# Three half tiles of an attention turned on VectorE, later stores of prepared weights, and banks planned to stay longer, in one core's attention with two MLPs

## The chip, the core and the metric

The kernel runs on one core of a Trainium2 chip. The metric is the device time of one execution in microseconds (us). The engines are TensorE (PE in the profile), VectorE (DVE), ScalarE (ACT), GpSimd (POOL) and SyncE (SP), which here only issues DMAs. ACT issues some DMAs too (ACTq in the rows).

## The reference

A two-stage attention feeds two gated MLPs; all of it is float32.

```python
def sm_attn(qq, kk, vv):                       # softmax attention, scale 1/8
    s = scale * np.matmul(qq, kk.transpose(0, 1, 3, 2))
    a = np.exp(s - np.max(s, axis=-1, keepdims=True))
    return np.matmul(a / (np.sum(a, axis=-1, keepdims=True) + 1e-09), vv)
# q, k, v: 8 batches x 8 heads x 576 x 64; p: 8 x 8 x 32 x 64
p_packed = sm_attn(p, k, v)
out = sm_attn(q, p_packed, p_packed)
x = out.transpose(0, 2, 1, 3).reshape(4608, 512)
x = silu(x @ w_in) @ w_out                     # 512 -> 2048 -> 512
x = hardswish(x @ w_in2) @ w_out2              # 512 -> 2048 -> 512, h * clip(h + 3, 0, 6) / 6
```

## The kernel before

**Tiles and blocks.** The attention is cut into 16 tiles, each of half a batch's heads; of q, k and v each tile has two half tiles of 128x512 values. The first MLP runs in nine blocks (`block`). In a block, `hidden(j, f, ...)` makes one of 16 groups of 128 hidden columns (PE lines L992 to L994, each float32 product being three passes: high by high, high by low, low by high), ACT applies SiLU (L1001) and makes its high half `gh` (L1008), VectorE the rest `gl` (L1009), and `project` (L1016 to L1018) multiplies them into four accumulators. The attention steps of coming tiles are run between these products. The second MLP runs last, from about 810 us to the end, with nothing else beside it.

**What orders the attention steps.** `Plan` counts products as its time. Each step has a due time and, if it needs PSUM, a number of banks out of a ring of four (`bank=`); `give` puts the bank back after an estimated hold. After the exponentials of a tile the plan takes it that banks come free later, by `LATE` = 24 (L820). So the order of all engines' work is fixed when the program is built; at run time an instruction only waits for what it needs.

**The attention steps that matter here.** `load_nat` (L367) loads the half tiles of q, k and v. `step_tr` (L451) turns one half tile of q or k: for tiles 0 to 3 by four PE transposes into one bank (L449) and an ACT copy out of it (T, L108), for tiles from 4 on by one VectorE transpose (L456). For that form the half tile has to lie otherwise in SBUF, so `load_nat` loads it by four DMAs of 32x16x32 values, 64 KB each, in place of two of 128x4x64 values, 128 KB each. The four are put in the list `due` and issued by `ask`; in blocks 0 and 1 `use` issues all that is in it at once. `step_kpq` turns the exponentials (L413, and T copied by ACT), and `step_pp` (L482, L485) multiplies them with v.

**Block 0** (about 36 to 145 us) also converts the first MLP's weights. For each group of w_in or w_out an ACT-issued DMA (`load_raw`, L155, 512 KB) brings the raw words; ACT (L180, L186), VectorE (L195, L199) and POOL (L208) turn the words into float32; ACT casts the high half (`conv_hi`, L219) and VectorE subtracts for the low half (`conv_lo`, L224), both into a tile `win` or `wo`. PE uses this tile in block 0, and SP stores it to DRAM for the later blocks (`keep`, L215, `w1i<-win` and `w1o<-wo`). There are three buffers for `win`: the cast of a group waits until the store of the group three before it has landed.

**DMA queues.** SP issues its DMAs in the program's order; so does ACT, between its other instructions. In the compiled program the DMAs of SP and ACT together take eight completion semaphores in turn, and an instruction that issues a DMA first waits until the DMA that had the semaphore before, eight issues earlier, has landed, unless another wait already implies it.

**Later blocks** read the stored weights back (`wi<-w1i` L247, `wo<-w1o` L260) and prepare the second MLP's weights: `Prep.all` works through 32 units, a `yield` at a time, each ending in three SP stores (L340 to L342) of the tiles `hi` and `c`, of which there are two buffers each.

Of the kernel before, what the change touches and what calls it, by code (L numbers as in the profile page):

```python
# [18 lines left out]
def tile_pack_attention_two_mlps(ctx: ExitStack, tc, q, k, v, p, w_in1, w_out1, w_in2, w_out2, out):  # L19
# [8 lines left out]
    nc = tc.nc  # L28
# [4 lines left out]
    P = 128  # L33
# [124 lines left out]
    def win_src(w, f):  # L158
        return w.bitcast(I32)[:, 2 * f * P:2 * (f + 1) * P].rearrange("(a p) f -> p a f", p=P)

    def wout_src(w, f):
        return w.bitcast(I32)[f * P:(f + 1) * P, :].rearrange("p (a f) -> p a f", a=1)
# [26 lines left out]
    def conv_begin(key, room=ring):  # L189
        conv_a(key, room)  # L190
        conv_b(key, room)

    def conv_shift(key):
        r = raws[key][1]
        nc.vector.tensor_scalar(out=r, in0=r, scalar1=3, scalar2=None, op0=ALU.logical_shift_left)  # L195

    def conv_sign(key):
        w1, r, t = raws.pop(key)
        nc.vector.scalar_tensor_tensor(out=r, in0=w1, scalar=-0x80000000, in1=r, op0=ALU.bitwise_and, op1=ALU.bitwise_or)  # L199
        raws[key] = r, t  # L200

    def conv_bits(key):
        conv_shift(key)
        conv_sign(key)
# [64 lines left out]
    class Prep:  # L269


        def __init__(self, pool, w_in, w_out_):
            self.pool = pool
            self.src = {"in": lambda f: win_src(w_in, f), "out": lambda f: wout_src(w_out_, f)}
            self.units = [(kind, f, h) for kind in ("in", "out") for f in range(HF) for h in range(2)]
            self.steps = self.all()

        def room(self):
# [22 lines left out]
        def all(self):  # L301
            self.load(0)
            for _ in range(6):
                yield
            for u, (kind, f, h) in enumerate(self.units):
                key = "p", u
                c = self.pool.tile([P, 8, P], F32, tag="c8", name="c8", bufs=2)
                hi = self.pool.tile([P, S7, P], F32, tag="hi7", name="hi7", bufs=2)
                conv_begin(key, self.room)
                yield  # L310
                yield
                conv_bits(key)
                yield
                if u + 1 < len(self.units):
                    self.load(u + 1)
                yield
                x, r = raws.pop(key)
                a = c[:, 0:4].bitcast(I32)
                if kind == "in":
                    x, r, a = x, r, a.rearrange("p n f -> p (n f)")  # L320
                else:
                    x, r = (t.rearrange("p (b r f) -> p b r f", b=8, r=2) for t in (x, r))
                    a = a.rearrange("p (r n) (b f) -> p (n b) r f", n=2, b=4)
                nc.gpsimd.tensor_add(out=a, in0=x, in1=r)
                yield

                nc.vector.tensor_add(out=c[:, 4], in0=c[:, 2], in1=c[:, 3])
                nc.vector.tensor_sub(out=c[:, 6], in0=c[:, 0], in1=c[:, 2])
                nc.vector.tensor_sub(out=c[:, 5], in0=c[:, 4], in1=c[:, 0])
                nc.vector.tensor_sub(out=c[:, 7], in0=c[:, 1], in1=c[:, 5])  # L330
                yield
                nc.scalar.copy(out=hi[:, 0:2].bitcast(F32R), in_=c[:, 0:2])
                nc.scalar.copy(out=hi[:, 2:7].bitcast(F32R), in_=c[:, 3:8])
                yield
                nc.gpsimd.tensor_sub(out=c[:, 0:2].bitcast(F32R), in0=c[:, 0:2], in1=hi[:, 0:2])
                nc.gpsimd.tensor_sub(out=c[:, 3:8].bitcast(F32R), in0=c[:, 3:8], in1=hi[:, 2:7])
                yield
                yield
                to = w2[kind][f].rearrange("s p f -> p s f")
                nc.sync.dma_start(out=to[:, :, h * P:(h + 1) * P], in_=hi)  # L340
                nc.sync.dma_start(out=to[:, 0:2, (2 + h) * P:(3 + h) * P], in_=c[:, 0:2])
                nc.sync.dma_start(out=to[:, 2:7, (2 + h) * P:(3 + h) * P], in_=c[:, 3:8])  # L342


    AHEAD = 3
# [5 lines left out]
    def ask(key=None):  # L351
        while due if key is None else any(k == key for k, _ in due):
            due.pop(0)[1]()
            if key is None:
                return
# [11 lines left out]
    def load_nat(n, what, j):  # L367
        src = {"k": k, "q": q, "v": v}[what]
        b, h0 = n // QPB, (n % QPB) * HQ + 2 * j
        m = half_kb(n, "nat", 2 * AHEAD, what)  # L370
        rows = src[b, h0:h0 + 2, 0:T, :]
        if what == "v":
            m = m.rearrange("p (h i d) -> p h i d", h=2, i=NI)
            load_queue[0].dma_start(out=m.rearrange("p h i d -> p h (i d)"), in_=rows.rearrange("h (p i) d -> p h (i d)", i=NI))
        elif n >= 4:

            g = m.rearrange("p (i b d) -> p i b d", i=NI, b=NI)
            for h in range(2):
                for e in range(2):
                    o = (2 * h + e) * NP  # L380
                    src = rows[h].rearrange("(b r i) d -> r i b d", b=NI, i=NI)[:, :, :, e * NP:(e + 1) * NP]
                    due.append(((what, n, j), lambda to=g[o:o + NP], src=src: nc.sync.dma_start(out=to, in_=src)))
        else:
            m = m.rearrange("p (i h d) -> p i h d", h=2, i=NI)
            for h in range(2):
                load_queue[0].dma_start(out=m[:, :, h, :], in_=rows[h].rearrange("(p i) d -> p i d", i=NI))
            m = m.rearrange("p i h d -> p i (h d)")
        nat[what, n, j] = m
# [58 lines left out]
    def turn_rows(ps, m):  # L447
        for i in range(NI):
            nc.tensor.transpose(ps[:, i * P:(i + 1) * P], m[:, i, :], ident)  # L449

    def step_tr(n, what, j):  # L451
        m = nat.pop((what, n, j))
        if n >= 4:
            ask((what, n, j))
            t = half_kb(n, "T", 5)
            nc.vector.transpose(out=t, in_=m)  # L456
            st[what, n, j] = t
            return
        ps = bank()
        turn_rows(ps, m)  # L460
        t = half_kb(n, "T", 5)
        copy(out=t, in_=ps)
        st[what, n, j] = t
# [260 lines left out]
    for j in range(2, B - 1):  # L724
        c, d = QPB * (j + 2), QPB * (j + 1)
# [26 lines left out]
    def use(what, n):  # L752
        used.add((what, n))
        load_next()
        while due and plan.block < 2:
            ask()
# [8 lines left out]
    class Plan:  # L765
# [40 lines left out]
        def run(self, step):  # L806
            self.steps.remove(step)
            _, key, cost, fn, _, tile, bank, count, also = step
            fn()
            self.now += cost  # L810
            for k in (key, *also):
                self.open.discard(k)
                self.done[k] = self.now
            if tile:
                self.tiles.append(tile)
            if bank:
                self.take(count)
                self.give(bank, count)
            if key[0] == "exps":
                self.late = self.now + LATE  # L820

        def tick(self, n, part, calm=False):
            self.now += n
# [16 lines left out]
    LATE = 24  # L840
# [3 lines left out]
    def window(c, d, b, a, j, x):  # L844
# [6 lines left out]
        def add(n, what, cost, fn, *need, tile=None, bank=5, also=(), count=1):  # L851
            if n is not None:
                steps.append(((what, n), cost, fn, need, tile, bank, [k for k in also if k[1] is not None], count))
# [30 lines left out]
        add(c, "spread", 0, lambda: spread_p(c), ("kpq", b), bank=0)  # L884

        def turn():
            add(d, "q0", 0, lambda: step_tr(d, "q", 0), (("t", b if j == 1 else None), 0), bank=5 if j == 0 and (d or 9) < 4 else 0, tile=("z", d))
            add(d, "q1", 0, lambda: [step_tr(d, "q", 1), use("q", d)], ("q0", d), bank=5 if j == 0 and (d or 9) < 4 else 0, tile=("z", d))
            add(a, "u", 0, lambda: [step_u(a), step_ut(a)], before[1], (("t", b), 22 if j else 0), bank=15)
            add(c, "k0", 0, lambda: step_tr(c, "k", 0), (("q1", d), 0), (("t", b if j == 1 and d is not None else None), 20), bank=5 if j == 0 and (c or 9) < 4 else 0, tile=("s", c))  # L890
            add(c, "k1", 0, lambda: [step_tr(c, "k", 1), use("k", c)], ("k0", c), bank=5 if j == 0 and (c or 9) < 4 else 0, tile=("s", c))

        if j == 0:
            if b is not None:
# [11 lines left out]
        else:  # L906
            p = pend.pop() if pend else None
# [11 lines left out]
            if keys:  # L919
                n_banks = (b is not None) + (p0 is not None) + 1  # L920
                add(keys[0][1], keys[0][0], 2 * n_banks, transposes, before[0] if b is not None else ("spread", c), ("spread", c), ("pp", p0), tile=b is not None and ("pp", b),
                    bank=8, count=n_banks, also=keys[1:])
# [13 lines left out]
            if keys:  # L936
# [3 lines left out]
                    bank=9, also=keys[1:], count=n_banks)  # L940
# [935 lines left out]
    for j in range(NBLK):  # L1876
        ws = WINDOWS[j] if j < len(WINDOWS) else []
        order = []
        n = QPB * (j + 1) - 1
# [13 lines left out]
        if j in mates:  # L1893
            for g in range(1, NG):
                fs = fuse_steps(j, g)
                lo, hi = [max(0, 18 * g * GF - 24) / (18 * NF) for g in (g - 1, g)]
# [101 lines left out]
```

## Time and profile before

| | |
|---|---|
| median of 3 runs (lowest to highest) | 1508.78 us (1508.05 to 1509.45) |
| profiled execution, its own time | 1509.61 us |
| its span in the trace | 1507.8 us |
| mean granted clock of TensorE | 0.995 of full speed |
| PE busy | 1483.1 us, 98% of the span |
| DVE / ACT / POOL busy | 1036.0 / 779.4 / 192.5 us |
| PE busy in 70:76 and 114:120 | 3.68 and 3.70 of 6.00 us |

A row of a timeline reads: start, duration (us), engine, line, operation, output<-input, and in square brackets the idle time of the engine just before it with what ended it. Several equal instructions in a row stand as one (x4). A matmul's duration is longer than its share of the engine, since matmuls overlap: the distance between starts tells what one costs. For a DMA issue (SPq, ACTq) the duration is that of issuing, not of the transfer; of several issues, their waits in between are in it.

### The profile page before, as it was taken

The page shows a single profiled execution, that of the slowest core. Times are in us where ns is not written, and L with a number is a line of the kernel's source. Part 1 is how long each engine was busy: PE and PEld are TensorE (multiplying, and loading weights), DVE is VectorE, ACT ScalarE, POOL GpSimd, SP SyncE. Part 2 cuts the span into 40 slices and gives each one's busy share as a digit, 9 for nine tenths or more (in the row PEclk, how much of TensorE's full clock was granted, in tenths as well). Part 3 has the DMA queues.
Part 4 walks back from the last instruction along what each step waited for, and adds up shares of the span by engine and source line. Part 5 has one row for each costly group of instructions (what it writes and reads, how often), then busy time and mean ns, then how long its engine had stood idle before and what let it go on. Part 6 is the DMA issues. An engine that isn't in the chain of part 4 may idle for free.

```text
span 1507.8 us, 21726 instructions
## 1 busy us (share of the span) xinstructions
PE 1483.1 (98%) x7550; PEld 1230.3 (82%) x7550; DVE 1036.0 (69%) x1695; ACT 779.4 (52%) x1241; POOL 192.5 (13%) x177
## 2 busy tenths in 40 slices
PE   7999999999999999999999999999999999999998
PEld 4777777777777778788878888888888888999998
DVE  6767466756575656653463779786978687778767
ACT  6876657655566456655452344334433443444443
POOL 2433011111211211123240000000000000000000
PEclk9999999999999999999999999999999999999999
DMA  9999789997698769868895576678667866997987
GB/s 246 306 306 276 247 214 253 274 253 198 177 245 263 199 165 306 231 178 239 243 291 178 193 225 216 195 216 252 219 193 223 242 215 210 286 313 255 271 273 226
DMA packets 434509, 358.52 MB, mean 238 GB/s; under 512 B 191200, under 2 KB 325856, under 8 KB 434400
## 3 DMA queue, kind: packets, MB, share of 16 engines
q1 hardware_dynamic: 422832, 343.59, 77.6%
q10 hardware_dynamic: 11568, 13.54, 2.9%
q8 instruction: 61, 1.00, 0.3%
q14 instruction: 48, 0.39, 0.1%
HBM read 295.17 MB, written 61.87 MB: 237 GB/s over the span
## 4 chain that ended last, share of the span: by engine, by line
PE 84%; ACT 6%; DMA 4%; DVE 3%; SPq 2%; issue 1%; POOL 1%; ACTq 0%; POOLq 0%; DVEq 0%
PE b L1270 8%; PE b L1268 8%; PE b L1269 8%; PE b L1363 8%; PE b L1366 7%; PE b L1365 7%; PE acc L1016 7%; PE acc L1017 7%; PE acc L1018 7%; PE hps L992 4%; PE hps L993 4%; PE hps L994 4%; DMA wo<-w1o 1%; DMA praw<-in_moe_w_out_dram 1%; PE abank L524 1%
## 5 line engine op out<-in xcount | busy, mean ns | idle before, releaser
L1009 DVE TENSOR_TENSOR gl<-hps,gh 128x512 fp32r<-128x512 f32 x144 | 98.9, 687 | 190.6 <-ACT gh L1008 187.8
L1366 PE MATMUL b<-ro,ws 128*128 128x512 f32 (+2 forms) x564 | 206.4, 366 | 0.0
L1365 PE MATMUL b<-ro,ws 128*128 128x512 f32 (+2 forms) x564 | 206.3, 366 | 0.0
L1268 PE MATMUL b<-xc,ws 128*128 128x512 f32 (+1 forms) x560 | 205.7, 367 | 0.0
L1270 PE MATMUL b<-xc,ws 128*128 128x512 f32 (+1 forms) x560 | 205.7, 367 | 0.0
L1269 PE MATMUL b<-xc,ws 128*128 128x512 f32 (+1 forms) x560 | 205.7, 367 | 0.0
L1311 DVE TENSOR_TENSOR ro<-g,ro 128x1024 fp32r<-128x1024 f32 (+1 forms) x140 | 161.5, 1158 | 41.5 <-ACT ro L1306 41.2
L1306 ACT CAST ro<-g 128x1024 fp32r<-128x1024 f32 (+1 forms) x140 | 132.0, 967 | 93.4 <-DVE g L1299 34.5
L1001 ACT ACTIVATE hps<-hps 128x512 f32<-128x512 f32 x144 | 83.9, 583 | 116.0 <-PE hps L994 115.0
L1363 PE MATMUL b<-ro,ws 128*128 128x512 f32 (+2 forms) x564 | 138.9, 367 | 0.3
L1366 PEld LDWEIGHTS b<-ro,ws 128*128 128x128 f32 x564 | 105.9, 188 | 13.1
L1365 PEld LDWEIGHTS b<-ro,ws 128*128 128x128 f32 x564 | 105.9, 188 | 13.1
L1268 PEld LDWEIGHTS b<-xc,ws 128*128 128x128 f32 x560 | 105.1, 188 | 13.2
L1269 PEld LDWEIGHTS b<-xc,ws 128*128 128x128 f32 x560 | 105.1, 188 | 13.2
L1016 PE MATMUL acc<-gh,wo 128*128 128x512 f32 x288 | 114.6, 398 | 1.3 <-DMA wo<-w1o 1.3
L1270 PEld LDWEIGHTS b<-xc,ws 128*128 128x128 f32 x560 | 105.1, 188 | 13.0
L1363 PEld LDWEIGHTS b<-ro,ws 128*128 128x128 f32 x564 | 102.9, 188 | 15.0 <-DVE ro L1311 2.1
L1016 PE MATMUL acc<-gh,wr 128*128 128x512 f32 x288 | 114.0, 396 | 0.5 <-ACT gh L1008 0.5
L1017 PE MATMUL acc<-gl,wr 128*128 128x512 f32 x288 | 112.5, 391 | 0.2 <-DVE gl L1009 0.2
L1018 PE MATMUL acc<-gh,wr 128*128 128x512 f32 x288 | 112.5, 390 | 0.0
L1018 PE MATMUL acc<-gh,wo 128*128 128x512 f32 x288 | 112.4, 390 | 0.0
L1017 PE MATMUL acc<-gl,wo 128*128 128x512 f32 x288 | 112.4, 390 | 0.0
(310 smaller groups left out, 2899.4 us busy)
## 6 DMA issues: line engine op xcount, KB each, us to landing
ws<-w2in SPq DMA_DIRECT2D x280, 256.0 KB, 3.3
ws<-w2out SPq DMA_DIRECT2D x280, 256.0 KB, 3.5
wi<-w1i SPq DMA_DIRECT2D x80, 512.0 KB, 6.6
wo<-w1o SPq DMA_DIRECT2D x64, 512.0 KB, 6.2
x1d<-x SPq DMA_DIRECT2D x18, 512.0 KB, 5.2
w1i<-win SPq DMA_DIRECT2D x16, 512.0 KB, 7.2
praw<-in_moe_w_in_dram SPq DMA_DIRECT2D x32, 256.0 KB, 6.2
praw<-in_moe_w_out_dram SPq DMA_DIRECT2D x32, 256.0 KB, 5.7
```

The source lines that it names most:

```text
L1009: nc.vector.tensor_sub(out=gl, in0=g, in1=f32(gh))
L1016: mm(acc[e], lhsT=w[:, 0, s], rhs=gh, start=first, stop=False)
L1017: mm(acc[e], lhsT=w[:, 0, s], rhs=gl, start=False, stop=False)
L1018: mm(acc[e], lhsT=w[:, 1, s], rhs=gh, start=False, stop=last)
L1268: mm(ps, lhsT=wh, rhs=xs[k][:, 0, c], start=first, stop=False, skip_group_check=True)
L1269: mm(ps, lhsT=wh, rhs=xs[k][:, 1, c], start=False, stop=False, skip_group_check=True)
L1270: mm(ps, lhsT=wl, rhs=xs[k][:, 0, c], start=False, stop=last, skip_group_check=True)
L1306: nc.scalar.copy(out=t[:, 0], in_=v)
L1311: nc.vector.tensor_sub(out=t[:, 1], in0=self.operand(s), in1=f32(t[:, 0]))
L1363: mm(to, lhsT=wh, rhs=x, start=False, stop=last, skip_group_check=True)
L1365: mm(to, lhsT=wh, rhs=x, start=first, stop=False, skip_group_check=True)
L1366: mm(to, lhsT=wl, rhs=x, start=False, stop=False, skip_group_check=True)
```

## The change

There are three parts.

1. q and k of tile 3 and q of tile 2 (six half tiles) are loaded by the four small DMAs each and turned on VectorE, as tiles 4 and up are. They need no bank any more. k of tile 2 stays on PE.
2. In `Prep.all` the three stores at the end of a unit are kept in a list and issued in the next unit, two `yield`s after its start.
3. After the exponentials of a tile in block 0 whose second exponential is none (the key's third entry is `None`), the plan takes banks to come free after 34 instead of 24.

```diff
@@ class Prep, all()
-                key = "p", u
+                key, after = ("p", u), self.after
                 conv_begin(key, self.room)
                 yield
                 yield
+                for fn in after:
+                    fn()
                 conv_bits(key)
...
                 to = w2[kind][f].rearrange("s p f -> p s f")
-                nc.sync.dma_start(out=to[:, :, h * P:(h + 1) * P], in_=hi)
-                nc.sync.dma_start(out=to[:, 0:2, (2 + h) * P:(3 + h) * P], in_=c[:, 0:2])
-                nc.sync.dma_start(out=to[:, 2:7, (2 + h) * P:(3 + h) * P], in_=c[:, 3:8])
+                self.after = [lambda o=o, i=i: nc.sync.dma_start(out=o, in_=i) for o, i in (
+                    (to[:, :, h * P:(h + 1) * P], hi), (to[:, 0:2, (2 + h) * P:(3 + h) * P], c[:, 0:2]), (to[:, 2:7, (2 + h) * P:(3 + h) * P], c[:, 3:8]))]
+            for fn in self.after:
+                fn()
@@ load_nat
-        elif n >= 4:
+        elif n >= 3 or (what, n) == ("q", 2):
@@ step_tr
-        if n >= 4:
+        if n >= 3 or (what, n) == ("q", 2):
@@ Plan.run
-                self.late = self.now + LATE
+                self.late = self.now + (34 if key[2] is None and not self.block else LATE)
@@ turn (q1 and k1 alike)
-            add(d, "q0", 0, lambda: step_tr(d, "q", 0), ..., bank=5 if j == 0 and (d or 9) < 4 else 0, tile=("z", d))
+            add(d, "q0", 0, lambda: step_tr(d, "q", 0), ..., bank=0, tile=("z", d))
-            add(c, "k0", 0, lambda: step_tr(c, "k", 0), ..., bank=5 if j == 0 and (c or 9) < 4 else 0, tile=("s", c))
+            add(c, "k0", 0, lambda: step_tr(c, "k", 0), ..., bank=5 if j == 0 and c == 2 else 0, tile=("s", c))
```

Lines after L276 have moved by one to four: L449, L482, L485 and L992 of before are L453, L486, L489 and L996 of the changed kernel, L382 (a small load) is L386, and L386 (a load of 128x4x64) is L390.

On PE, in block 0 between two projects (72 to 81 us in the trace of before), there stood before, `nat` being a half tile of q or k as loaded, `abank` a PSUM bank, `T` turned rows:

```order
L449 MATMUL abank<-ident,nat 128x128 x4
L992 MATMUL hps<-xh_546,win 128x512
L993 MATMUL hps<-xl_553,win 128x512
L994 MATMUL hps<-xh_546,win 128x512
L992 MATMUL hps<-xh_559,win 128x512
L993 MATMUL hps<-xl_561,win 128x512
L994 MATMUL hps<-xh_559,win 128x512
L482 MATMUL abank<-nat,T 32x64 x16
L485 MATMUL abank<-vt,a1Tt 32x64 x4
L449 MATMUL abank<-ident,nat 128x128 x8
L992 MATMUL hps<-xh_563,win 128x512
```

and now:

```order
L996 MATMUL hps<-xh_555,win 128x512
L997 MATMUL hps<-xl_557,win 128x512
L998 MATMUL hps<-xh_555,win 128x512
L996 MATMUL hps<-xh_559,win 128x512
L997 MATMUL hps<-xl_563,win 128x512
L998 MATMUL hps<-xh_559,win 128x512
L486 MATMUL abank<-nat,T 32x64 x16
L489 MATMUL abank<-vt,a1Tt 32x64 x4
L1020 MATMUL acc_578<-gh,wr_886 128x512
```

All transposes of this place are gone (four more stood in the project behind it), and pp of tile 2 (L482, now L486) has moved behind the last part of the hidden group. The other place that loses transposes, 110 to 119 us, loses two groups of four.

On SP, at the start of block 0 (30 to 50 us), there stood before, `nat<-in_q_dram` being the load of q of tile 2, `nat<-in_k_dram` that of k of tile 3, `w1i_117<-win` the stores of converted w_in:

```order
L386 DMA nat<-in_q_dram 128x4x64 x4
L155 DMA raw<-in_moe_w_in_dram 128x4x256
L393 DMA pn<-in_p_dram 128x64
L155 DMA raw_233<-in_moe_w_out_dram 128x1024
L215 DMA w1i_117<-win 256x4x128
L386 DMA nat<-in_k_dram 128x4x64 x4
L215 DMA w1i_117<-win 256x4x128
```

and now:

```order
L155 DMA raw<-in_moe_w_in_dram 128x4x256
L397 DMA pn<-in_p_dram 128x64
L155 DMA raw_229<-in_moe_w_out_dram 128x1024
L386 DMA nat<-in_q_dram 32x16x32 x5
L215 DMA w1i_117<-win 256x4x128
L386 DMA nat<-in_q_dram 32x16x32 x3
L386 DMA nat<-in_k_dram 32x16x32 x8
L215 DMA w1i_117<-win 256x4x128
```

Eleven loads stand between the first two weight stores, where there were four.

Also on SP, at 78 to 96 us, `nat<-in_q_dram` being q of tile 3 and `nat<-in_k_dram` k of tile 4, before:

```order
L374 DMA nat<-in_v_dram 128x2x256 x2
L386 DMA nat<-in_q_dram 128x4x64 x4
L382 DMA nat<-in_k_dram 32x16x32 x8
L215 DMA w1o_123<-wo 128x2x512
L215 DMA w1i_119<-win 256x4x128 x2
```

and now:

```order
L378 DMA nat<-in_v_dram 128x2x256 x2
L386 DMA nat<-in_q_dram 32x16x32 x8
L386 DMA nat<-in_k_dram 32x16x32 x8
L215 DMA w1o_123<-wo 128x2x512
L215 DMA w1i_119<-win 256x4x128 x2
```

Sixteen loads stand ahead of the next weight stores, where there were twelve. In the compiled program the DMA ahead of which a queue has to wait for a landing changes with them: before the `w1o_123` store of the changed kernel SP waits for the raw load that ACT issues last before it (at 95.66 us in the trace of before), while before it waited for one of the k loads.

On VectorE six transposes `T<-nat` are new (four around 75 to 83 us, two around 110 to 120 us), on ACT six copies `T<-abank` are gone. In blocks 1 to 8 each group of three stores of part 2 stands later on SP by one to some twenty DMAs; the group at 224 us stands now behind the next tile's loads of v, q and k, which it stood ahead of.

## Rows read from the trace of the kernel before

**Rows 1.** The page, part 1: busy time of each engine.

```profile
PE 1483.1 (98%) x7550; PEld 1230.3 (82%) x7550; DVE 1036.0 (69%) x1695; ACT 779.4 (52%) x1241; POOL 192.5 (13%) x177
```

**Rows 2.** PE's waits, whole span: line <- what ended them: total us, times, longest.

```profile
PE abank L449 <- DVE gl L1009: 4.6, 2, 2.3
PE abank L482 <- DMA nat<-in_v_dram: 1.7, 2, 0.9
```

**Rows 3.** Timeline of PE, first place with transposes.

```profile
74.32 0.66 PE L449 MATMUL abank<-ident,nat 128*128 128x128 f32 x4 [2.32 <-DVE gl L1009]
...
76.88 1.08 PE L482 MATMUL abank<-nat,T 128*32 128x64 f32 x32
...
81.33 0.40 PE L1018 MATMUL acc<-gh,wr 128*128 128x512 f32 x1
...
82.24 0.39 PE L1017 MATMUL acc<-gl,wr 128*128 128x512 f32 x1
...
83.39 0.39 PE L992 MATMUL hps<-xh,win 128*128 128x512 f32 x1
```

**Rows 4.** Windows: PE, PEld, DVE, ACT, POOL busy (count), granted clock, DMA share, GB/s.

```profile
76.00:82.00 6.00, 6.00 (x65) 4.59 (x63) 4.19 (x8) 5.24 (x10) 2.87 (x2) 0.75 0.87 278
```

**Rows 5.** Timeline of DVE, both places.

```profile
73.58 0.69 DVE L1009 TENSOR_TENSOR gl<-hps,gh 128x512 fp32r<-128x512 f32 x1 [1.09 <-ACT gh L1008]
...
117.77 0.69 DVE L1009 TENSOR_TENSOR gl<-hps,gh 128x512 fp32r<-128x512 f32 x1 [1.56 <-ACT gh L1008]
```

**Rows 6.** Groups by line: count, busy us, mean ns of one, idle before.

```profile
L456 DVE STREAM_TRANSPOSE T<-nat 128x512 f32<-128x512 f32 x48 | 31.6, 688 | 2.3 <-DMA nat<-in_k_dram 2.3
```

**Rows 7.** Timeline of SP, 30 to 48 us.

```profile
30.82 2.63 SPq L386 DMA_DIRECT2D nat<-in_q_dram  x4
...
41.40 5.89 SPq L386 DMA_DIRECT2D nat<-in_k_dram  x4
47.39 0.62 SPq L215 DMA_DIRECT2D w1i<-win  x1
```

**Rows 8.** Timeline of ACT and its queue, 48 to 75 us.

```profile
48.08 0.34 ACTq L155 DMA_DIRECT2D raw<-in_moe_w_out_dram  x1
...
54.82 0.62 ACT L219 CAST win<-cr 128x512 fp32r<-128x512 f32 x1 [1.09 <-DMA w1i<-win]
...
74.17 0.58 ACT L108 COPY T<-abank 128x512 f32<-128x512 f32 x1
```

**Rows 9.** DMA issues of 48.05:48.3: count, KB each, us from issue to landing.

```profile
raw<-in_moe_w_out_dram ACTq DMA_DIRECT2D x1, 512.0 KB, 6.3
```

**Rows 10.** Timeline of PE, later hidden groups and the second pp.

```profile
57.93 0.39 PE L992 MATMUL hps<-xh,win 128*128 128x512 f32 x1
...
108.11 0.39 PE L992 MATMUL hps<-xh,win 128*128 128x512 f32 x1
...
120.93 1.08 PE L482 MATMUL abank<-nat,T 128*32 128x64 f32 x32
```

**Rows 11.** Timeline of SP, 82 to 97 us.

```profile
82.94 8.99 SPq L382 DMA_DIRECT2D nat<-in_k_dram  x8
92.49 1.92 SPq L215 DMA_DIRECT2D w1o<-wo  x1
94.50 1.78 SPq L215 DMA_DIRECT2D w1i<-win  x2
```

**Rows 12.** Timeline of ACT and its queue, 92 to 105 us.

```profile
92.25 0.62 ACT L219 CAST wo<-cr 128x512 fp32r<-128x512 f32 x1 [1.45 <-DMA nat<-in_k_dram]
...
95.66 0.39 ACTq L155 DMA_DIRECT2D raw<-in_moe_w_in_dram  x1
...
103.52 0.39 ACTq L155 DMA_DIRECT2D raw<-in_moe_w_in_dram  x1
103.95 0.62 ACT L219 CAST win<-cr 128x512 fp32r<-128x512 f32 x1 [2.78 <-POOL cr L208]
```

**Rows 13.** DMA issues of 94.4:94.6, columns as in group 9.

```profile
w1i<-win SPq DMA_DIRECT2D x1, 512.0 KB, 9.0
```

**Rows 14.** Timeline of SP, stores of part 2 and the loads behind them.

```profile
227.23 2.32 SPq L342 DMA_DIRECT2D w2in<-c  x1
229.76 0.60 SPq L364 DMA_DIRECT2D vt<-in_v_dram  x1
230.42 1.64 SPq L374 DMA_DIRECT2D nat<-in_v_dram  x2
```

More of the change, by code (lines that the diff above doesn't have):

```diff
@@ L275, in __init__ @@
             self.units = [(kind, f, h) for kind in ("in", "out") for f in range(HF) for h in range(2)]
+            self.after = []
             self.steps = self.all()
@@ L886, in turn @@
         def turn():
-            add(d, "q0", 0, lambda: step_tr(d, "q", 0), (("t", b if j == 1 else None), 0), bank=5 if j == 0 and (d or 9) < 4 else 0, tile=("z", d))
-            add(d, "q1", 0, lambda: [step_tr(d, "q", 1), use("q", d)], ("q0", d), bank=5 if j == 0 and (d or 9) < 4 else 0, tile=("z", d))
+            add(d, "q0", 0, lambda: step_tr(d, "q", 0), (("t", b if j == 1 else None), 0), bank=0, tile=("z", d))
+            add(d, "q1", 0, lambda: [step_tr(d, "q", 1), use("q", d)], ("q0", d), bank=0, tile=("z", d))
             add(a, "u", 0, lambda: [step_u(a), step_ut(a)], before[1], (("t", b), 22 if j else 0), bank=15)
-            add(c, "k0", 0, lambda: step_tr(c, "k", 0), (("q1", d), 0), (("t", b if j == 1 and d is not None else None), 20), bank=5 if j == 0 and (c or 9) < 4 else 0, tile=("s", c))
-            add(c, "k1", 0, lambda: [step_tr(c, "k", 1), use("k", c)], ("k0", c), bank=5 if j == 0 and (c or 9) < 4 else 0, tile=("s", c))
+            add(c, "k0", 0, lambda: step_tr(c, "k", 0), (("q1", d), 0), (("t", b if j == 1 and d is not None else None), 20), bank=5 if j == 0 and c == 2 else 0, tile=("s", c))
+            add(c, "k1", 0, lambda: [step_tr(c, "k", 1), use("k", c)], ("k0", c), bank=5 if j == 0 and c == 2 else 0, tile=("s", c))
         if j == 0:
```

## The prediction

> **What bounds the kernel now.** I read the busy times first: PE works 98% of the span [rows 1], so nearly everything that the change can gain is PE idle time or PE work that goes away, and what it can lose is new idle time of PE. Next, PE's waits. The two largest behind the start, and the two that the change aims at, are 4.6 us in front of transposes (L449), two times 2.3 us, both ended by VectorE's gl, and 1.7 us in front of pp for v [rows 2]. Then the timelines of those places, and last, since DMAs are what the change adds, SP and ACT's queue in block 0. There the reader is to see that SP's stores of converted weights decide when ACT may go on: its cast of 54.82 waited 1.09 us for a store issued at 47.39 [rows 7, 8].
>
> **Part 1, what it takes away.** One group of four transposes costs PE 82.24 − 81.33 = 0.91 less two matmul steps of 0.23, so 0.455 us [rows 3]; six groups make 2.7 us. The stalls: in front of L449 PE idles until 74.32 because the bank is the one that gl reads, which ends at 73.58 + 0.69 = 74.27 [rows 3, 5]. pp takes over that bank's place and also needs T, copied by ACT until 74.17 + 0.58 = 74.75 [rows 8]. So pp can start at 74.8 in place of 76.88. Between the start of pp and the next hidden group at 83.39 lie 6.51 us; of these the transposes go (at least 3 × 0.455 = 1.37), and the hidden part that now stands ahead of pp (3 × 0.23 = 0.68): 4.46 remain, the group starts at 79.3, 4.1 us earlier. In the second place gl ends at 118.46 and T, by the first place, 0.48 later, at 118.95, against pp at 120.93 [rows 5, 10]: 2.0 us, and 2.5 with the ACT copy (0.58) that is gone ahead of it. If nothing else came later, part 1 would give 4.1 + 2.5 = 6.6 us. The clock adds little: it was 0.75 after the stall [rows 4], but the remaining wait for T is nearly as long, so I count nothing, with 0.5 us either way in the range.
>
> VectorE gets six transposes of 0.688 [rows 6], 4.1 us; ACT loses six copies of about 0.58, 3.5 us. VectorE waited 1.09 and 1.56 us for ACT just in front of the two gl that count [rows 5], which is what hides them; without that cover one transpose in front of pp's end would cost 0.7. I count nothing.
>
> **Part 1, what it puts in the way.** The loads cost twice the issues. On SP the four loads of q of tile 2 took 2.63 us, 0.66 each [rows 7]; eight small ones of k took 8.99, 1.12 each with their waits [rows 11]. Two stores stand behind them.
>
> *First store.* Before, k of tile 3 was issued from 41.40 on in four DMAs, which ended only at 47.29, since the last waited for the landing of a raw load (the eight semaphores), and the store followed at 47.39 [rows 7]. In the changed program this same wait stands ahead of the second of eleven loads, and a later one, for ACT's raw load of 48.08, ahead of k's sixth. That raw load landed at 48.08 + 6.3 = 54.4 [rows 8, 9]. Three loads follow, 0.66 to 1.12 each: the store goes at 56.4 to 57.8, and with the 7.4 us that it took before (47.39 to the cast it released at 54.82) lands at 63.8 to 65.2. ACT's cast goes from 54.82 to about 64, so ACT is late by D = 9. Bounds: ten more loads than before lie between the first landing and the store; at 0.66 and with no second landing to wait for they make 6.6, at 1.12 they make 11.2; I take 5.5 to 11. PE has only 57.93 − 55.44 = 2.5 us of slack to this cast [rows 8, 10]; it idles for the other 6.5. ACT has next to no idle time until T at 74.17 to make it good, at most 1 us, so pp starts at 74.8 + 8 = 82.8, and the group of 83.39 at 87.3: minus 4.1 has become about +4 us. Queued behind the store on SP are p, k's tail and the next weight stores; behind the waiting cast on ACT, the raw loads, SiLU and the exponentials.
>
> *Second store.* Before `w1o` SP waited for a k load and issued at 92.49, then `w1i` at 94.50 [rows 11]. That landed 9.0 later, at 103.5 [rows 13], which is when ACT's queue, and then its cast, went on (103.52, 103.95) [rows 12]: this store already sets ACT's pace. Now `w1o` has to wait for ACT's raw load of 95.66 to land. That load was itself held by SP (the 1.45 us of idle at 92.25 [rows 12]), so alone it might go at 95.2; with PE late by 4 it goes at about 99. Plus 6.3 (the raw load's landing) is 105.3, `w1i` 0.7 to 2.0 later at 106.5, landing 9.0 later at 115.5 (7.4, as the other store: 113.9). The cast of 103.95 comes at 115.5, 11.5 late. PE has 108.11 − 104.57 = 3.5 us of slack there [rows 10, 12], so it stalls again. From that cast to gl ACT shows no idle time, only the copy that is gone, so pp comes at 118.95 − 0.58 + 11.5 = 129.9, against 120.93: block 0 ends 9 us later, the 6.6 us being in this already. Bounds: with D = 5.5, the raw load at 96 and the shorter times the landing is at 110.4, pp at 124.8, +4; with D = 11 and a 9.0 us landing, +11. I take +8, a little under the middle working, since ACT has some idle time between 85 and 95 and loses four copies there.
>
> After this PE has no stall in which it could make time good: the rest of block 0 and all that follows shifts as a whole.
>
> **Part 2.** The three stores waited on SP for ACT and POOL; at 224 us the last of them took 2.32 us at 227.23, and v was issued behind them only at 230.42 [rows 14]. pp stalled 1.7 us for that v [rows 2]. In the new order v stands ahead of the stores, so this goes: −1.7. The stores wait less, since their tiles have long been ready; queued behind them now are praw and wo loads, and `hi` and `c`, with two buffers each, come free later, by one unit out of two. Nearest rows for a harm: the same two waits of 0.8 us, moved to another load. Bounds: −3 to +1.7. I take −1.7.
>
> **Part 3** moves no work but pp of tile 2 behind one hidden part, which is counted above.
>
> **Sum.** +8 − 1.7 = +6.3 us on the profiled execution's 1509.61; the median is 0.8 lower, so 1508.8 + 6.3 = 1515. Its own range is 1508 (+4 − 3 − 2 for what I may have missed in ACT's recovery) to 1521 (+11 + 1.7).
>
> **Rivals.**
> *The issues hide (A).* If the loads and the raw landings ahead of the two stores are over as early as before, ACT is not delayed and part 1 gives its 6.6: 1508.8 − 6.6 − 1.7 = 1500.5, faster. It decides at the first store: ACT's cast may slip 2.5 us before PE idles, so the store would have to go by 50. For it: SP had no more than 0.66 us per load when nothing waited, and the 5.89 us of [rows 7] were mostly waiting. Against: the waits are for landings, which no faster issue brings forward. The Trainium skill (DMA: Bandwidth & Descriptors, "Issuing engines are not separate DMA queues") says that the time a sequencer takes to start a DMA is usually small against the DMA itself; by it the added issues would be nearly free and the sum that of A. The rows agree for an issue alone (0.66 against 6.3) but show waits between issues that the rule leaves out.
>
> *Only the second store is late (B).* If the raw load lands early enough that D stays under 2.5, PE and ACT reach 95 us about 2 us early; the raw load at 93.7 lands at 100, `w1i` at 101.3 lands at 110.3, the cast is 6.3 late and pp comes at 124.7: +3.8 − 1.7 = +2.1, 1511. For it: raw loads land in less than 6.3 when few others run. Against: few others never run there; the DMA share was 0.87 even in the window shown [rows 4].
>
> *That the change doesn't do what it says* is out: all 24 transposes are gone from PE's compiled order.
>
> **How the numbers follow.** The two stores late: 64%. A: 21%. B: 15%. A run can tell about 0.2%, 3 us, from no change, so faster means under 1505.8, slower over 1511.8. The likeliest case is slower in 0.85 of its share, same in 0.13, faster in 0.02; A is faster in 0.95, else same; B same in 0.7, slower in 0.25, faster in 0.05. Sums: slower 0.54 + 0.04 = 0.58, same 0.08 + 0.01 + 0.105 = 0.20, faster 0.01 + 0.20 + 0.01 = 0.22. The predicted time is the likeliest case's, 1515. Cases of both signs hold weight; the likeliest one's own range is 1508 to 1521. For 8 in 10 the range reaches into A: 1502 (leaving out some 13% of A's lower part) to 1521 (leaving out some 6%).
>
> **What would show it.** Right, if in the changed kernel: SP issues the second `w1i` store of block 0 at 56 to 58 in place of 47.39; an ACT win cast near 55 waits some 9 us for DMA w1i<-win; PE idles 5 to 7 us before a hidden group near 58 to 65; no PE wait in front of transposes by gl is left; `w1o` at 92.49 goes after 101; a second ACT cast waits for w1i<-win until after 110; pp of tile 3 starts at 125 to 131 instead of 120.93; around 235 the 1.7 us for v are gone. Wrong, if the cast at 55 waits under 2.5 us: then A or B, told apart by the second cast. Should pp of tile 3 come before 119 and the end still be no earlier, part 2 has cost what part 1 gave.

## The result, and the profile after

The changed kernel takes 1519.45 us (median of 6 runs, 1516.41 to 1524.72), the kernel before 1508.5 beside it: a ratio of 1.0073 [1.006, 1.0085], 10.95 us slower. The profiled execution took 1520.24, its span is 1518.5. PE has less to do and yet ends later, so the difference is idle time of PE and a lower clock behind some of it. The page, part 1, against [rows 1]:

```profile
PE 1481.6 (98%) x7526; PEld 1229.0 (81%) x7526; DVE 1039.7 (68%) x1701; ACT 776.1 (51%) x1235; POOL 192.7 (13%) x177
```

PE's waits of the whole span (line <- what ended them: total us, times, longest), against [rows 2]:

```profile
PE hps L996 <- ACT win L219: 5.9, 2, 3.1
...
PE abank L486 <- ACT T L108: 3.9, 1, 3.9
...
PE abank L686 <- DMA wi<-w1i: 2.0, 1, 2.0
PE abank L417 <- ACT d L471: 1.9, 1, 1.9
...
PE abank L620 <- ACT d L108: 1.6, 1, 1.6
```

The 4.6 us for gl in front of transposes and the 1.7 for v are gone. New are 5.9 us for ACT's casts of w_in, 3.5 for ACT's d behind them, 3.9 for T and 2.0 for a weight load. Where the casts come from is on SP. Its timeline (start, duration of the issue with its wait), against [rows 7] and [rows 11]:

```profile
32.92 4.95 SPq L386 DMA_DIRECT2D nat<-in_q_dram  x5
...
47.52 8.70 SPq L386 DMA_DIRECT2D nat<-in_k_dram  x8
56.32 0.63 SPq L215 DMA_DIRECT2D w1i<-win  x1
...
84.44 9.35 SPq L386 DMA_DIRECT2D nat<-in_q_dram  x8
94.35 9.52 SPq L386 DMA_DIRECT2D nat<-in_k_dram  x8
104.51 1.55 SPq L215 DMA_DIRECT2D w1o<-wo  x1
106.16 1.77 SPq L215 DMA_DIRECT2D w1i<-win  x2
```

The store of 47.39 now goes at 56.32, that of 92.49 at 104.51. What held SP is seen from two landings of ACT's raw loads (DMA issues: count, KB each, us from issue to landing), the first issued at 47.84, the second at 97.68:

```profile
raw<-in_moe_w_out_dram ACTq DMA_DIRECT2D x1, 512.0 KB, 6.4
...
raw<-in_moe_w_in_dram ACTq DMA_DIRECT2D x1, 512.0 KB, 6.8
```

They land at 54.2 and 104.5. SP issues the sixth load of k at 54.28, two more and the store behind it, and `w1o` at 104.51: these are the two waits that the prediction named. ACT and its queue at the two casts behind them, and at the T copy for pp of tile 3, against [rows 8] and [rows 12]:

```profile
52.88 0.39 ACTq L155 DMA_DIRECT2D raw<-in_moe_w_in_dram  x1
60.21 0.62 ACT L219 CAST win<-cr 128x512 fp32r<-128x512 f32 x1 [6.74 <-DMA pn<-in_p_dram]
60.35 0.34 ACTq L155 DMA_DIRECT2D raw<-in_moe_w_out_dram  x1
...
112.75 0.62 ACT L219 CAST win<-cr 128x512 fp32r<-128x512 f32 x1 [8.40 <-DMA w1i<-win]
...
127.58 0.62 ACT L219 CAST win<-cr 128x512 fp32r<-128x512 f32 x1 [1.58 <-POOL pl L658]
128.10 0.58 ACT L108 COPY T<-abank 128x512 f32<-128x512 f32 x1
```

The row at 60.21 names a load of p, which a cast has no use for; the store of 56.32 landed 3.8 us after its issue, at 60.1, and frees the cast's buffer. It comes 5.4 us later than before (54.82), the second 8.8 (103.95). And PE (its timeline), against [rows 3] and [rows 10]:

```profile
60.88 0.79 PE L996 MATMUL hps<-xh,win 128*128 128x512 f32 x1 [3.05 <-ACT win L219]
...
64.14 1.12 PE L620 MATMUL abank<-tails,ppf 128*128 128x64 f32 x4 [1.62 <-ACT d L108]
...
113.42 0.50 PE L996 MATMUL hps<-xh,win 128*128 128x512 f32 x1 [2.88 <-ACT win L219]
...
119.47 0.66 PE L417 MATMUL abank<-ident,d 128*128 128x128 f32 x4 [1.87 <-ACT d L471]
...
128.74 0.89 PE L486 MATMUL abank<-nat,T 128*32 128x64 f32 x32 [3.91 <-ACT T L108]
...
268.98 0.77 PE L686 MATMUL abank<-wi,ph 128*128 128x512 f32 x1 [1.97 <-DMA wi<-w1i]
```

pp of tile 3 is 7.8 us late (128.74 against 120.93). The same product with vt behind the next pp is 9.75 late (185.72 against 175.97), the wait for wo 7.8 (256.89 against 249.13, the stall for v between them being gone), and the place at 312 us 11.1, of which 10.7 are left at the end. So the loss has two places: block 0, and a new wait for wi at 269 us.

### The profile page after: what moved, and what is told of

The parts are those of the page before. It is cut to its first block, busy times and chain, and to the rows that moved or that the text cites. A ratio compares the mean times of both kernels' runs of the same rounds, so it can differ in the third digit from the quotient of the medians.

```text
span 1518.5 us, 21702 instructions
## 1 busy us (share of the span) xinstructions
PE 1481.6 (98%) x7526; PEld 1229.0 (81%) x7526; DVE 1039.7 (68%) x1701; ACT 776.1 (51%) x1235; POOL 192.7 (13%) x177
## 2 busy tenths in 40 slices
DMA packets 440844, 358.51 MB, mean 236 GB/s; under 512 B 197536, under 2 KB 332192, under 8 KB 440736
## 4 chain that ended last, share of the span: by engine, by line
PE 84%; DMA 5%; ACT 5%; DVE 3%; SPq 1%; issue 1%; POOL 1%; ACTq 0%; POOLq 0%; DVEq 0%
PE b L1273 8%; PE b L1274 8%; PE b L1272 8%; PE b L1367 8%; PE b L1370 7%; PE b L1369 7%; PE acc L1020 7%; PE acc L1022 7%; PE acc L1021 7%; PE hps L996 4%; PE hps L998 4%; PE hps L997 4%; DMA wi<-w1i 2%; DMA nat<-in_k_dram 1%; PE abank L686 1%
## 5 line engine op out<-in xcount | busy, mean ns | idle before, releaser
L1022 PE MATMUL acc<-gh,wr 128*128 128x512 f32 x288 | 112.7, 391 | 0.0
```

The lines of the kernel that those rows point to most:

```text
L1022: mm(acc[e], lhsT=w[:, 1, s], rhs=gh, start=False, stop=last)
```

## The experiments

All ratios are to the kernel before, measured beside each; 0.001 is 1.5 us. "Part 1" here is the turn with its loads and plan, part 2 the later stores. Differences in us are taken from the ratios.

| run | kernel | median, us | ratio |
|---|---|---|---|
| | the changed kernel | 1519.45 | 1.0073 [1.006, 1.0085] |
| e1_stores | before + part 2 | 1512.04 | 1.0024 [1.0013, 1.0035] |
| e2_turn | changed without part 2 | 1517.95 | 1.006 [1.0045, 1.0075] |
| e3_loads | before + twelve DMAs more | 1515.36 | 1.0043 [1.0028, 1.0058] |
| e4_two | changed, loads as before | 1510.66 | 1.0014 [1.0004, 1.0024] |
| e11_turn_two | e2, loads as before | 1508.71 | 1.0 [0.9991, 1.0009] |
| e12_one | before with six DMAs fewer | 1507.13 | 0.998 [0.9971, 0.999] |
| e5_stores_first | e2, stores ahead of the loads | 1513.17 | 1.0033 [1.0017, 1.005] |
| e8_paced | e2, loads one by one | 1511.73 | 1.0023 [1.0013, 1.0034] |
| e6_q2k3 | e2, only q2 and k3 | 1518.82 | 1.0071 [1.0048, 1.0095] |
| e7_q3 | e2, only q3 | 1513.28 | 1.0032 [1.0015, 1.005] |
| e9_pool_loads | before, the loads on POOL | 1533.15 | 1.0159 [1.0144, 1.0173] |
| e10_turn_pool | e2, the loads on POOL | 1564.42 | 1.0371 [1.0357, 1.0385] |

### The parts alone

e1_stores is the kernel before with part 2, e2_turn the changed kernel without it.

```diff
-                nc.sync.dma_start(out=to[:, :, h * P:(h + 1) * P], in_=hi)
...
+                self.after = [lambda o=o, i=i: nc.sync.dma_start(out=o, in_=i) for o, i in (
...
+                for fn in after:
+                    fn()
```

> The kernel before with part 2 alone (prepared weights' stores issued two steps later). Theory (the small loads on SP cost the time): the two PE waits for v of 1.7 us around 235 us go, block 0 stays as before; 1506 to 1509 us. Rival (part 2 makes the loss, by what is queued behind the later stores): most of the 11 us, 1516 to 1520 us.

> The changed kernel without part 2: six half tiles by small loads and VectorE, banks held 34, stores of prepared weights where they were. Theory: all of the loss is here, with PE idle near 61, 113 and 129 us as in the changed kernel and the 1.7 us for v back; 1518 to 1523 us. Rival (part 2 makes the loss): 1504 to 1510 us.

Part 2 alone costs 3.6 us (0.0024), where the prediction had −1.7; part 1 alone costs 9.1. e1 lies between both of its ranges, e2 just under its theory's. In e1 the stall for v is gone, but PE, in its timeline, waits twice for wi instead:

```profile
258.51 0.47 PE L686 MATMUL abank<-wi,ph 128*128 128x512 f32 x1 [1.45 <-DMA wi<-w1i]
...
276.89 0.47 PE L686 MATMUL abank<-wi,ph 128*128 128x512 f32 x1 [1.70 <-DMA wi<-w1i]
```

SP of before at that place (timeline; `w2in` are the stores of part 2, `wi` the four loads that PE needs from 258 us on):

```profile
249.57 5.00 SPq L247 DMA_DIRECT2D wi<-w1i  x4
255.09 0.37 SPq L340 DMA_DIRECT2D w2in<-hi  x1
```

and of e1:

```profile
242.69 0.42 SPq L343 DMA_DIRECT2D w2in<-hi  x1
243.21 1.94 SPq L343 DMA_DIRECT2D w2in<-c  x2
...
251.74 2.37 SPq L247 DMA_DIRECT2D wi<-w1i  x4
```

The group of stores of 224 us left its place ahead of v and took one ahead of the four wi loads, where none had stood (the next group, at 255.09, came behind them). The loads begin 2.2 us later, while PE, 1.7 us of stall richer, wants them 2.2 us earlier (its preceding use of wi is at 256.19 in place of 258.41). How much of the wait is the queue's, the landing of the first of the four tells (DMA issues), before and in e1:

```profile
wi<-w1i SPq DMA_DIRECT2D x1, 512.0 KB, 8.5
...
wi<-w1i SPq DMA_DIRECT2D x1, 512.0 KB, 6.6
```

It lands at 258.1 before and at 258.3 in e1, and before PE used it at 259.11, 1.0 us after the landing. So most of the wait of 1.45 is the time won at v, come back at the next landing. The second wait, 1.70, is for a load issued 0.1 us later than before (269.15 against 269.04) which lands in 7.6 us in place of 6.1; why it lands later is not shown. In the changed kernel the first of the two is there: stores at 252.32, the loads at 261.39, the wait at 268.98.

### The loads without the turn, and the turn without the loads

e3_loads is the kernel before, its transposes on PE, with the six half tiles loaded by four DMAs of 64x4x64 each in the places and order of the changed kernel.

```diff
+                if n >= 3 or (what, n) == ("q", 2):
+                    for e in range(2):
+                        due.append(((what, n, j), lambda to=m[e * 64:e * 64 + 64, :, h, :], ...: nc.sync.dma_start(out=to, in_=src)))
```

> The kernel before, with the same six half tiles loaded by four DMAs of 64x4x64 (64 KB) in place of two, in the changed kernel's SP order, but turned on PE and ACT as before; no part 2, no part 3. Theory: the order of SP alone delays the weight stores, so ACT's casts near 55 and 104 us come 5 to 9 us late without any gain from the transposes; 1517 to 1524 us. Rival (VectorE's transposes or the moved pp make the loss): 1507 to 1511 us.

Timeline of SP and of ACT in e3:

```profile
49.61 5.25 SPq L389 DMA_DIRECT2D nat<-in_k_dram  x8
54.95 0.63 SPq L215 DMA_DIRECT2D w1i<-win  x1
```

```profile
60.66 0.62 ACT L219 CAST win<-cr 128x512 fp32r<-128x512 f32 x1 [5.73 <-DMA w1i<-win]
```

The same bytes in twelve more DMAs, at the places of the changed kernel, cost 6.5 us (0.0043), 0.54 for each; the first store and its cast are about as late as in the changed kernel. The time lies between the theory's range and the rival's; the late cast is the theory's. Two things are not parted here. Three loads of q also moved behind the first store, so that number and place go together. And the changed kernel's loads are in shorter pieces (its page has 440844 packets, e3's 434701), which may belong to the 2.6 us between e3 and e2. The other way round, e4_two is the changed kernel and e11_turn_two the kernel e2, both with two DMAs for each of the six half tiles at their old place.

```diff
-        elif n >= 3 or (what, n) == ("q", 2):
+        elif n >= 4:
...
-            nc.vector.transpose(out=t, in_=m)
+            nc.vector.transpose(out=t, in_=m if n >= 4 else m.rearrange("p i d -> p (i d)"))
```

> The changed kernel with the six half tiles loaded as before, by two DMAs of 128x4x64 each at the old place (what VectorE turns is then not the right rows; all instructions and sizes stay). Theory: SP's order in block 0 is that of before, the casts near 55 and 104 us wait no longer, and the gain of the transposes shows: 6.6 + 1.7 us, 1499 to 1503 us. Rival (VectorE's transposes or the moved pp make the loss): 1515 to 1521 us.

> The changed kernel without part 2, with the six half tiles loaded by two DMAs each, as before and at their old place, and turned by VectorE all the same; the rows then lie otherwise, so that what is turned is not the right part of q and k, and the output differs. It is the turn without its loads. Theory (the second place is paced by ACT, which is paced by the stores, so that the two gains do not add): 1506 to 1508.5, pp of tile 3 near 120. Rival (the full 6.6 us of the prediction's first sum are there once the loads cost nothing): 1500 to 1503, pp of tile 3 near 114 to 116.

Without its loads the turn is worth nothing that can be measured (1.0, at most 1.4 us either way); e11 lies at the upper end of its theory's range. Between e2 and e11 lie 9.1 us, which are the loads. e4 missed both of its ranges: it is 2.1 us [0.6, 3.6] slower than before, and as e11 is e4 without part 2, that is part 2's.

Why the 6.6 us are not there is seen in e11. At the first place the gain came: the hidden group of 83.39 starts at 79.68, 3.7 us earlier (4.1 was said), although the cast of 54.82 is 1.2 us late in this execution (55.99). At the second place PE (timeline) reaches pp early and waits:

```profile
119.16 1.08 PE L482 MATMUL abank<-nat,T 128*32 128x64 f32 x32 [4.25 <-ACT T L108]
```

and ACT (timeline), up to that T:

```profile
102.34 0.62 ACT L219 CAST win<-cr 128x512 fp32r<-128x512 f32 x1 [2.22 <-DMA w1i<-win]
...
110.97 0.62 ACT L219 CAST win<-cr 128x512 fp32r<-128x512 f32 x1 [1.40 <-POOL cr L208]
...
113.62 0.62 ACT L219 CAST wr<-cr 128x512 fp32r<-128x512 f32 x1 [0.91 <-DMA w1i<-win]
...
118.52 0.58 ACT L108 COPY T<-abank 128x512 f32<-128x512 f32 x1
```

T comes at 118.52, before at 118.17, although PE had been ahead and ACT had one copy fewer: what ACT won, it spent on waiting for stores and for converted words, 4.5 us in the three rows, against 2.78 in the same stretch before [rows 12]. pp moves from 120.93 to 119.16, 1.8 us, and the granted clock is 0.52 in 118:124 behind the wait (0.72 in 120:126 before), so that the wi product of 141.07 comes 0.4 us late (141.49). e4 shows the same wait (4.89 for T at 119.92). The time won at the first place does not reach the second, since the second is paced by ACT and ACT by SP's stores.

e12_one goes the other way: the kernel before with one DMA in place of two for each of the six half tiles.

```diff
+        elif n >= 3 or (what, n) == ("q", 2):
+            load_queue[0].dma_start(out=m.rearrange("p (h r) -> p h r", h=2), in_=rows.rearrange("h (p i) d -> p h (i d)", i=NI))
+            m = m.rearrange("p (i d) -> p i d", i=NI)
```

> The kernel before with one DMA in place of two for each of the six half tiles: the rows lie otherwise in the tile, so that what is turned is not the right part of q and k, and the output differs; TensorE turns them as before. Six DMAs fewer on SP in block 0, the same bytes. Theory (a DMA more or less ahead of a store is worth 0.5 to 0.75 us of SP's queue, and the store's landing sets ACT's casts): the store of 47.39 goes at 44 or earlier, the casts no longer wait, 1505 to 1508. Rival (only what exceeds the slack of before costs; there is nothing to gain below): 1509, no change.

Timeline of SP and of ACT in e12:

```profile
42.39 2.89 SPq L384 DMA_DIRECT2D nat<-in_k_dram  x2
45.37 0.61 SPq L215 DMA_DIRECT2D w1i<-win  x1
```

```profile
54.57 0.62 ACT L219 CAST win<-cr 128x512 fp32r<-128x512 f32 x1
```

The store goes 2.0 us earlier, less than the theory's 3.4, the cast no longer waits, and the time falls by 1.5 to 4.4 us, as the theory had it. So from six DMAs fewer to twelve more the time rises with their number, with PE turning all the while; in e12 the pieces are longer too (429805 packets against 434509 before).

### Where the delay sits on SP

e5_stores_first is e2 with waiting stores issued ahead of each burst of small loads in block 0; e8_paced is e2 with the loads issued one by one instead of in a burst.

```diff
+        if due and plan.block == 0:
+            keep(1)
```

```diff
-        while due and plan.block < 2:
+        while due and plan.block == 1:
```

> The changed kernel without part 2, with one thing more: in block 0, before the small loads are issued in one go, SP issues the weight stores that are waiting (all but the newest). Same DMAs, same sizes, other order on SP. Theory (the order on SP makes the loss): the store of 56 us goes before 50, that of 106 us before 90, ACT's casts wait under 2 us, and 1504 to 1510 us comes out. Rival (the small loads cost by their number and pieces on the DMA engines, wherever they stand): 1515 us or more.

> The changed kernel without part 2, the small loads of block 0 issued one by one between the products instead of in one go at the end of q's step. Theory: the second weight store goes some 5 us earlier than in the changed kernel, and the stores near 106 us stand ahead of most loads; 1506 to 1512 us. Rival (small loads cost wherever they stand): 1515 us or more.

Timeline of SP in e5:

```profile
48.41 0.63 SPq L215 DMA_DIRECT2D w1i<-win  x1
49.14 9.65 SPq L382 DMA_DIRECT2D nat<-in_k_dram  x8
...
62.88 0.62 SPq L215 DMA_DIRECT2D w1i<-win  x1
```

The first store is back at 48.41, its cast at 55.58. But the burst takes 9.65 us in its new place too, and the next store goes at 62.88 instead of 50.14; its cast at 66.66 waits 6.01 us. The delay is handed on to the next store, and a little under half of the loss returns (4.1 us); the time lies between the theory's range and the rival's. Paced, the loads come between the stores, no cast of the first place waits more than 2.5 us, and 5.6 us return, within the theory's range; 3.5 us stay.

e6_q2k3 and e7_q3 are e2 with only q of tile 2 and k of tile 3, or only q of tile 3, turned (the conditions in `load_nat`, `step_tr` and the banks are cut to these).

```diff
-        if n >= 3 or (what, n) == ("q", 2):
+        if n >= 4 or (what, n) == ("q", 3):
```

> The changed kernel without part 2, q of tile 3 loaded and turned as before: only the first burst of small loads is there. Theory (either late store costs about half): ACT's cast near 60 us waits over 5 us, the one near 104 to 108 little; 1511 to 1515 us. Rival (only the second store decides, since ACT makes good what the first took): 1507 to 1510 us.

> The changed kernel without part 2, q of tile 2 and k of tile 3 loaded and turned as before: only the second burst of small loads is longer than before. Theory (either late store costs about half): the cast near 55 us as before, the one near 104 us waits for w1i<-win some 5 us; 1511 to 1514 us. Rival (the first store makes the whole loss): 1506 to 1510 us.

With q3 alone the first place is as before (store at 49.32, its cast waiting 0.84) and the second is late: the store of 92.49 goes at 99.31, the cast at 108.04 waits 7.22 us, and the time is 4.8 us [2.3, 7.5] longer, as the theory had it. With q2 and k3 alone the store goes at 56.36 and the time is as long as with all six, 10.7 us [7.2, 14.3], more than either range of e6 allowed. Turning q3 costs 4.8 us alone and, within some 4 us, nothing beside the others; as with the gains, the two places do not add.

### Another queue

e9_pool_loads is the kernel before with the twelve loads issued on POOL's queue, one by one; e10_turn_pool is e2 with its 24 there.

```diff
-                load_queue[0].dma_start(out=m[:, :, h, :], in_=rows[h].rearrange("(p i) d -> p i d", i=NI))
+                src = rows[h].rearrange("(p i) d -> p i d", i=NI)
+                if n >= 3 or (what, n) == ("q", 2):
+                    due.append(((what, n, j), lambda to=m[:, :, h, :], src=src: nc.gpsimd.dma_start(out=to, in_=src)))
...
```

> The kernel before with one edit: the two loads of each of the six half tiles (q and k of tile 3, q of tile 2) are issued on GpSimd's queue, one at a time through block 0, in place of SP's burst. All is computed as before, TensorE turns the tiles. SP loses twelve issues in block 0. Theory (SP's queue, through the landings that it waits for, sets when stores go and so when ACT casts): the casts that waited 1.1 and 1.5 us for stores no longer wait, and the time is 1504 to 1508. Rival (the queue is not the limit; an issue on GpSimd delays its conversions of weights): 1511 or more, with PE waiting for c or hi of POOL in block 0.

> The changed kernel without part 2 (stores where they were), with the small loads of q and k of tile 3 and q of tile 2 issued on GpSimd's queue, one at a time through block 0, in place of SP's burst. All is computed as before. Theory (the loss of the turn is the stores that stand behind its loads on SP): 1504 to 1509, against 1517.95 with the burst on SP. Rival (the doubled number of small transfers costs on any queue): 1513 or more.

Both are much slower, by 24 and 56 us, and both theories fail. SP was relieved (in e9 none of these loads stands ahead of a store), but POOL converts weights. Its timeline in e9, and the landing of the load of 46.95 (DMA issues):

```profile
46.95 0.76 POOL L388 DMA_DIRECT2D nat<-in_q_dram  x1 [4.75 <-issue]
50.74 0.75 POOL L388 DMA_DIRECT2D nat<-in_q_dram  x1 [3.03 <-issue]
53.53 0.75 POOL L388 DMA_DIRECT2D nat<-in_q_dram  x1 [2.04 <-issue]
54.29 2.49 POOL L208 TENSOR_TENSOR cr<-cr 128x512 int32<-128x512 int32 x2
```

```profile
nat<-in_q_dram POOLq DMA_DIRECT2D x1, 128.0 KB, 3.5
```

Between these loads (the first is at 41.28) POOL passes 2.8 to 5.7 us. The next goes 0.3 us after the one before has landed: the load of 46.95 lands at 50.4, and the next is at 50.74; that one lands in 2.5, at 53.2, and the next is at 53.53. The conversions that stand behind these loads in POOL's order, at 46.45 before, come at 54.29; ACT's cast at 55.60 waits 9.83 us for them. So another queue with an engine behind it on ACT's path asked more than SP's. The remedy failed by a cost of its own, and says nothing for or against the cause of the loss. e10 lies in its rival's range, but e9, with no more loads than before, is slow too.

## Why the prediction was right, and where its steps were off

**Right: the mechanism and its places.** Slower, because more loads ahead of two weight stores hold up ACT's casts. The stores go at 56.32 (56 to 58 was said) and at 104.51 and 106.16 (105.3 and 106.5); the casts wait 6.74 and 8.40 us; pp of tile 3 starts at 128.74 (129.9 in the middle working, 125 to 131 in the list), the wait for gl is gone, the stall for v too. Rivals A and B fall: the first cast slips 5.4 us, over the 2.5 at which both begin. The Trainium skill (DMA: Bandwidth & Descriptors, "Issuing engines are not separate DMA queues") says that the time on the sequencer to start a DMA is usually small against the DMA itself. The trace agrees for one issue that waits for nothing, 0.63 us at 56.32 against 3.8 to land. The price of the queue is not in that rule: e3's twelve DMAs cost 0.54 us each at the end of the kernel, and SP stood waiting for landings until 54.28 and 104.51.

One reading of the second place was too simple. [rows 12] put the cast at 103.95 down to POOL's cr, ready at 103.92, 0.4 us after the store's landing; so before the change the store did not set that cast alone. In the changed kernel cr is ready at 107.09 and the store lands at 112.7, so there it does: POOL alone would have made the cast 3.2 us late, the store makes it 8.8.

**Too large: the landings.** For the first store 7.4 us was taken over from before; it was 3.8. So D is 5.4, just under the lower bound of 5.5, and PE idles 4.7 us (3.05 and 1.62), not 6.5. For the second, 9.0 was taken and 6.5 came. The windows tell what differs (PE, PEld, DVE, ACT, POOL busy, clock, DMA share, GB/s): before, from issue to landing,

```profile
47.40:54.80 7.40, 7.40 (x35) 5.53 (x36) 5.29 (x10) 5.00 (x10) 4.58 (x4) 1.00 1.02 299
```

and after:

```profile
56.30:60.20 3.90, 1.52 (x7) 0.94 (x5) 0.00 (x0) 0.00 (x0) 0.00 (x0) 1.00 0.90 208
```

In the changed kernel all stand waiting for this store, ACT issues no raw load between 52.88 and 60.35, and 208 GB/s move instead of 299. A delay on the queue thins the traffic that its own transfers compete with; that this is the cause is argued from these rows and was not tried apart.

**Too large: the 6.6 us of part 1.** The step that failed adds 4.1 and 2.5 "if nothing else came later". e11 has the loads as before, and 0 [−1.4, 1.4] is what part 1 gives. The 4.1 of the first place came (3.7 in e11); it is not kept at the second. The wait for gl hid one for T, which the prediction saw at the first place and took to move along at the second; but there T hangs on ACT's queue, and that on stores. The same chain gave +1.6 in the changed kernel: from the cast at 112.75 to pp are 16.0 us, not the 14.4 taken over, since ACT waits 1.58 for POOL at 127.58. As this cast came 2.8 us earlier than taken (112.75 against 115.5), pp comes out only 1.2 us off: two terms were wrong in opposite senses, and that they nearly cancel is luck.

**Wrong in sign: part 2.** −1.7 was taken, with +1.7 as the upper end; e1 measured +3.6 [2.0, 5.3]. The 1.7 at v came. The step that failed took it as kept: it named what is queued behind the stores at their new place (praw and wo) and did not look at wi, of which four loads stood there and whose landing left 1.0 us of room before. In the changed kernel PE waits 1.97 for it at 268.98, and the granted clock is lower behind that (window):

```profile
268.00:280.00 12.00, 11.02 (x42) 8.99 (x43) 8.77 (x17) 5.38 (x11) 2.63 (x3) 0.86 1.04 336
```

12 us at 0.86 are 1.7 us; together 3.6, against the 3.3 by which the lateness grows from 256.89 (7.8) to 312 us (11.1). The same stretch of before (258:270) had a clock of 1.00.

**Part 3** does what the prediction said: with 24 in place of 34 the changed kernel's order differs on PE alone, where pp of tile 2 then stands ahead of the last part of its hidden group, as it did before the change. No run has this order, so what part 3 is worth by itself is not shown.

**Sum.** +8 and −1.7 were taken; pp of tile 3 is 7.8 late, then 2.0 are added by 185 us, 2.0 taken back at v and 3.3 added at wi, which makes the 11.1. Of the first 2.0 some 1.1 are small waits of PE between 140 and 186 us; the rest was not followed up. So +6.3 was forecast and 11.0 came, near the upper end of the range: part 1 cost 9.1 in place of 8, and part 2 cost 3.6 in place of giving 1.7. Alone the parts make 12.7, which the noise (1.6 to 2.3 us either way for each) does not part from the 11.0 of both.

## What to carry to other kernels

Before loads are split to spare an engine, look at what stands behind them on the issuing queue, and follow that to the engine which waits for it; here 2.7 us of transposes and two visible stalls were traded against two stores that pace another engine. Gains at two places of one chain add only if what paces the second is not paced itself by something that the change leaves as it was; ask that of each wait that stands right behind the one removed. When a store is moved out of one load's way, list every load between its old and its new place, and ask how much room the next landing leaves; here 1.0 us, and the 1.7 won came back as a wait with a lower clock behind it.

## What the runs showed of the hardware

A 512 KB store took 3.8 us to land with 208 GB/s moving and 7.4 with 299. A load on POOL's queue was followed by the next only 0.3 us after it had landed, for the first four 2.8 to 5.7 us after its issue, where SP issued the next after 0.63 to 0.68 when nothing held it (47.52, 48.15 and 48.83 in the changed kernel). And a stall of PE can cost more than itself: behind the two of 3.05 and 1.62 us the clock was 0.70 for six us, part of it at the lower of its two levels of 1.2 and 2.4 GHz (window of the changed kernel):

```profile
64.00:70.00 6.00, 5.86 (x21) 4.94 (x22) 5.08 (x10) 5.00 (x12) 3.62 (x3) 0.70 1.07 356
```

Not each does: around those of 2.88 and 1.87 us the clock was 1.00 in 112:118 and 118:124.
